# A fused attention and two-layer expert kernel: other step numbers for its planner, and two kinds of subtraction and rounding on other engines

## The chip, the cores and the metric

One Trainium2 chip, one of its cores. The metric is the device time of one execution in microseconds, the median of several runs; the kernel before has 794.7 us, median of three runs (794.32 to 796.21). Tensors lie in SBUF on 128 partitions; TensorE (PE, weight loads PEld) writes to PSUM; VectorE (DVE), ScalarE (ACT) and GpSimd (POOL) work between them; SyncE (SP) issues most DMAs.

## What is computed

Three layers one behind the other, on 1536 tokens (2 batches of 768) of 512 numbers:

```
attention, 8 heads of 64:  scores = q k' / 8, kept where the 6-bit hash of q equals that of k
                           (the signs of q @ proj and k @ proj), else -1e9; softmax; @ v
first layers:              h = x @ w_in (512 x 2048); g = h * sigmoid(1.702 h); x = g @ w_out (2048 x 512)
experts, 8 of 512x1024x512: logits = x @ w_gate + log1p(exp(x @ w_noise)) * noise; the two best per token,
                           softmax of the two; sum of weight * relu(x @ w1[e]) @ w2[e]
```

Matrices are split into a high and a low part of 16 bits, and a product is three matmuls: high by high, high by low, low by high.

## The kernel before, in words

**Steps.** The work is laid out in steps g, from about -17 to 116, in the loop of `fused` that ends with `by_turns`. Attention takes steps 0 to 95, one for each block of 128 queries of a head: batch b, chunk cc of 256 queries (three in a batch), pair hp of heads, head h and tile t. In a step come the score matmuls of step g+2 (`qk`, L259), the row maximum of step g+1 on VectorE (`rowmax`, L271), the exponential on ScalarE (`expo`, L280), and for steps under 24 a transpose on TensorE (`e_turn`, L298) and copies on ScalarE (L306). From step 24 on the probabilities are split into two 16-bit parts (`e_hi`, L319, ScalarE; `e_lo`, L328, VectorE) and transposed by a DMA (L332). `pv` (L373; L366 in the early steps) multiplies by the values some steps after a unit of four. A score tile has two PSUM buffers, so `qk` waits for the row maximum of two steps before.

**Keys and queries.** `stacks` puts the stages of one key or query tile on steps: `load`, `stack_hi` (rounding, L152; remainder on GpSimd, L154; scaled copy, L158 or L160), `stack_lo` (L167, and the DMA transpose L178), `buckets` (hash matmuls L195 and L196, copied to a tile `pc` by ScalarE, L200), `one_hot` (two comparisons on VectorE, L206) and `stack_end` (L213, and the second transpose L214). Their steps come from the tables KA (keys) and QA (queries); HE says which engine rounds, PC how many `pc` buffers there are. VA and VF set the steps of the values (`v_hi`, `v_lo`, `v_load32`).

**First layers.** The 32 weight blocks, 16 of `w_in` and then 16 of `w_out`, come as 8-byte numbers, 512 KB a block: `w_load` (L423), `w_bits` (three VectorE operations that make 4-byte numbers, L433, L436, L439), `w_split` (scaling on GpSimd, L452; high part on ScalarE, L455; low part on GpSimd, L456). Table W gives the step of each; its load comes two steps before. The raw numbers of the first 16 lie where the parts of `w_out` come later; those of the last 16 share three buffers (`wraw`). Each of six chunks of 256 tokens takes 16 steps behind its attention: in pieces 0 to 7 `moe_pe` computes h (L476), ScalarE takes a tanh (L494), VectorE multiplies (L506), ScalarE rounds (L520) and the lower part is subtracted (`moe_split`, L522) by the engine that GS names; in pieces 8 to 15 it multiplies by `w_out` (L487).

**Routing.** `route` computes the gate (L627, L629) of a chunk from rows transposed by a DMA (L589), some 30 small VectorE operations, and scatters the rows to the experts' slots in DRAM by indirect DMAs of GpSimd (L736). RA gives its first step, counted from the first step of the chunk. The slots are cleared beforehand from step I0 on, the output from step O0 on.

**Order.** Up to step 99 a planner of the language chooses each engine's order when the program is built: it takes what is ready by its own estimate of times, earlier steps first. Each engine then runs its instructions in that fixed order, each waiting for what it needs. From step 100 on the order is the program's. The experts come after step 116: `l1` (L854), `l1_out` (L864, L865), `l2` (L885, L879), `l2_out` (L895), and an indirect DMA that adds to the output (L902).

The tables are set like this (only the last update of W is quoted), and `stacks` uses them:

```
PARAM.update(W=[(g_,1) for g_ in [-6,-4,-2,0,2,3,4,5,7,8,9,10,12,13,14,15,17,18,19,20,20,21,21,22,22,23,23,24,24,25,25,26]])
...
        oh = PARAM["OH"]
        at(g - 2, load, nm, b, u)
        at(g, stack_hi, nm, b, u)
        soon(g + 1, stack_lo, nm, b, u)
        start(g + PARAM['BK'], buckets, nm, b, u)
        at(g + oh, one_hot, nm, b, u)
        soon(g + oh + 1, stack_end, nm, b, u)
```

Of the kernel before, what the change touches and what calls it, by code (L numbers as in the profile page):

```python
# [57 lines left out]
PARAM = dict(GM=16, HE=lambda nm, b: 'D', OE=lambda nm, b: 'D', SC=lambda nm, b: 'D', WB=0, XO=lambda b: 'D', NG=16, WS=lambda i: 'P', TS=lambda g: True, XL=lambda g: 'D', GW=2, E0=7, T0=12, T1=16, EL=8, WX=3, PV={(1,2,3):4}, PVD=5, ST={}, VA={}, RA={}, O0=48, OS=2, IS=2, FU=16, VF=2, EC=lambda g: 'AA', QX=8, QS=3, EA=1, S1=(8,8,8,9,9,9,11,13), QE=8, XG=2, XB=2, PC=2, OH=3, BK=3, R0=18, R1=0, LK=8, WL=1, NW=3, LE=lambda nc: nc.scalar, I0=24, LQ=8, LV=0, W=[(g, 1) for g in range(-6, 30)], KA={(0,0,0):-8,(0,0,1):-6,(0,1,0):-4,(0,1,1):-2}, QA={(0,0,0):-7,(0,0,1):-3}, HI=lambda g: 'P', LO=lambda g: False)  # L58
# [10 lines left out]


PARAM.update(W=[(g_,1) for g_ in [-6,-4,-2,0,2,3,4,5,7,8,9,10,12,13,14,15,17,18,19,20,20,21,21,22,22,23,23,24,24,25,25,26]])


@with_exitstack
# [1185 lines left out]
```

## Time and profile before

| what | value |
|---|---|
| median of 3 runs | 794.7 us (794.32 to 796.21) |
| the profiled execution | 792.2 us, span of its instructions 790.5 us |
| granted TensorE clock, mean | 0.976 of 2.4 GHz |
| busy: PE, DVE, ACT, POOL | 705.3, 496.9, 444.0, 282.1 us |
| row maxima of the 96 attention steps | 22.4 to 447.2 us |
| experts' matmuls | about 512 to 775 us |

The profile is of one execution. A busy time is the union of an engine's instructions in a stretch. A wait is the idle time of an engine before an instruction, put down to what ended it last. A granted clock of 0.50 is 1.2 GHz, of 1.00 is 2.4 GHz.

### The profile page before, as it was taken

To read this page: it belongs to the slowest core of one execution; us is meant where nothing else is said; L and a number is where in the kernel's file an instruction comes from. 1 tells how busy PE (TensorE), PEld (TensorE's weight loads), DVE (VectorE), ACT (ScalarE), POOL (GpSimd) and SP (SyncE) were. 2 spreads that over 40 slices of the span, in tenths; PEclk is the share of its full clock that TensorE was granted. 3 is DMA by queue.
4 is the path that set the end of the run, shared out by engine and by line. 5 is a ranking of instruction groups with operands and counts; after the bars stand their busy time and mean duration, and the time that the engine had idled before them with its cause. 6 is when DMAs were issued, how large, how long until landed. Compare 5 with 4: busy or idle time off the path is not lost.

```text
span 790.5 us, 14896 instructions
## 1 busy us (share of the span) xinstructions
PE 705.3 (89%) x5432; PEld 432.6 (55%) x5433; DVE 496.9 (63%) x1245; ACT 444.0 (56%) x958; POOL 282.1 (36%) x360
## 2 busy tenths in 40 slices
PE   1786689997888899889999999999999999999995
PEld 0453357555654575467557667466554545555452
DVE  8689689857985687378768725665643526345220
ACT  3678977657785686477658614445543534435220
POOL 7456856822462356114222224222031221302203
PEclk9999889999999999999999999999999999999998
DMA  8999657999999999975697580658977668484213
GB/s 196 224 250 317 195 175 167 274 255 171 170 198 194 170 194 217 177 137 103 117 178 133 107 290 11 187 194 209 280 120 242 193 121 267 61 255 85 27 17 45
DMA packets 254973, 136.83 MB, mean 173 GB/s; under 512 B 211696, under 2 KB 230704, under 8 KB 254896
## 3 DMA queue, kind: packets, MB, share of 16 engines
q1 hardware_dynamic: 248880, 122.68, 66.3%
q0 software_dynamic: 6016, 13.16, 9.4%
q8 instruction: 43, 0.70, 0.3%
q14 instruction: 34, 0.28, 0.1%
HBM read 62.27 MB, written 23.20 MB: 108 GB/s over the span
## 4 chain that ended last, share of the span: by engine, by line
PE 44%; DVE 4%; issue 1%; DMA 1%; ACT 1%; POOL 1%; POOLq 0%; DVEq 0%; ACTq 0%
PE ph L854 15%; PE py L885 14%; PE px L487 7%; PE h L476 3%; DMA et<-er 1%; PE pv L373 1%; PE py L879 1%; PE s L259 1%; DVE er L328 1%; POOL out_dram L902 1%; DVE ew L794 1%; DVE th L506 0%; ACT er L319 0%; DVE e L271 0%; ACT ew L793 0%
## 5 line engine op out<-in xcount | busy, mean ns | idle before, releaser
L476 PE MATMUL h<-xt,wi 128*128 128x256 f16 x1152 | 136.9, 274 | 5.9 <-DVE th L506 4.0
L487 PE MATMUL px<-wo,gt 128*128 128x512 f16 x576 | 133.2, 384 | 2.0 <-ACT wo L455 1.1
L854 PE MATMUL ph<-xg,ew 128*128 128x400 f16 (+2 forms) x864 | 132.8, 314 | 1.0 <-DVE ht L865 1.0
L794 DVE SCALAR_TENSOR_TENSOR ew<-w,ew 128x1024 f16<-128x1024 f32 x64 | 77.8, 1225 | 83.3 <-ACT ew L793 83.3
L885 PE MATMUL py<-ew,ht 128*128 128x512 f16 x576 | 126.0, 379 | 0.0
L476 PEld LDWEIGHTS <-wi 128*128 128x128 f16 x1152 | 111.9, 98 | 25.3 <-issue 8.0
L902 POOL DMA_INDIRECT out_dram<-yo,ti x32 | 54.0, 1687 | 200.5 <-ACT yo L895 190.9
L259 PE MATMUL s<-kt,qt 128*128 128x512 f16 (+3 forms) x384 | 84.3, 340 | 31.7 <-DVE e L271 24.3
L854 PEld LDWEIGHTS <-ew 128*128 128x128 f16 x864 | 80.4, 98 | 51.0 <-issue 2.8
L328 DVE SCALAR_TENSOR_TENSOR er<-e,mx,er 128x768 f16<-128x768 f32 x68 | 71.6, 1055 | 51.2 <-ACT er L319 50.2
L522 POOL TENSOR_TENSOR gt<-th,gt 128x512 f16<-128x512 f32 x48 | 57.0, 1188 | 105.5 <-ACT gt L520 105.5
L885 PEld LDWEIGHTS <-ht 128*128 128x128 f16 x576 | 56.1, 98 | 67.0 <-issue 0.2
L271 DVE TENSOR_SCALAR_CACHE_REDUCE e<-s 128x768 f32<-128x768 f32 x96 | 90.5, 948 | 3.2 <-PE pt L298 1.3
L487 PEld LDWEIGHTS <-gt 128*128 128x128 f16 x576 | 55.5, 98 | 66.4 <-issue 5.4
L280 ACT ACTIVATE e<-e,mx 128x768 f32<-128x768 f32 x96 | 89.4, 931 | 1.8
L319 ACT ACTIVATE er<-e,mx 128x768 f16<-128x768 f32 x68 | 63.1, 930 | 36.1 <-DMA et<-er 28.2
L895 ACT ACTIVATE yo<-py,wv 128x512 f32<-128x512 f32 x24 | 16.5, 687 | 94.6 <-PE py L885 57.9
L259 PEld LDWEIGHTS <-qt 76*128 76x128 f16 (+1 forms) x384 | 35.0, 100 | 61.2 <-issue 26.7
L793 ACT ACTIVATE ew<-w 128x1024 f16<-128x1024 f32 x64 | 66.2, 1048 | 0.1
L864 ACT ACTIVATE ht<-ph 128x400 f16<-128x400 f32 (+2 forms) x72 | 33.4, 465 | 57.7 <-PE ph L854 57.1
L865 DVE SCALAR_TENSOR_TENSOR ht<-ph,ht 128x400 f16<-128x400 f32 (+2 forms) x72 | 37.5, 523 | 30.7 <-ACT ht L864 30.6
L373 PE MATMUL pv<-et,vt 128*64 128x256 f16 x648 | 44.0, 277 | 6.5 <-DMA et<-er 6.3
(233 smaller groups left out, 918.8 us busy)
## 6 DMA issues: line engine op xcount, KB each, us to landing
w<-in_moe_w_dram SPq DMA_DIRECT2D x64, 512.0 KB, 5.4
wo<-in_moe_w_in_dram SPq DMA_DIRECT2D x16, 512.0 KB, 5.1
wraw<-in_moe_w_out_dram SPq DMA_DIRECT2D x16, 512.0 KB, 5.0
slots<-blank SPq DMA_DIRECT2D x6, 1032.0 KB, 6.3
v<-in_v_dram SPq DMA_DIRECT2D x28, 192.0 KB, 4.1
out_dram<-zeros SPq DMA_DIRECT2D x13, 256.0 KB, 3.3
k<-in_k_dram SPq DMA_DIRECT2D x16, 192.0 KB, 2.9
q<-in_q_dram SPq DMA_DIRECT2D x24, 128.0 KB, 2.9
```

The costliest lines, as they stand in the source:

```text
L259: nc.tensor.matmul(ps[:, n0 * 128:n1 * 128], qt[:kr, s, h, t, :], kt[:kr, s, h, n0:n1, :].rearrange("p c t -> p (c t)"), start=(s == 0), s ...
L271: nc.vector.tensor_scalar(e32, st[g]["ps"][:, :S], -FAR, -TOP, op0=OP.max, op1=OP.max, accum_out=mx[:, 0:1])
L280: nc.scalar.activation(e32, e32, AF.Exp, scale=0.125, bias=st[g]["mx"][:, 1:2], accum_out=sms[b, cc, hp][:, 2 * h + t:2 * h + t + 1] if g ...
L319: nc.scalar.activation(er[:, 0], st[g]["e"], AF.Copy, scale=r)
L328: nc.vector.scalar_tensor_tensor(er[:, 1], d["e"], d["mx"][:, 3:4], er[:, 0], op0=OP.mult, op1=OP.subtract)
L476: nc.tensor.matmul(ph[:, a, :], wi[ws][:, d, f0:f0 + 128], xt[:, d, xs, :], start=(d == 0 and ws == 0 and xs == 0), stop=(d == HP - 1 and ...
L487: nc.tensor.matmul(px, gts[ci, f // 2][:, gs, f % 2, t * 128:t * 128 + 128], wo[ws][:, f, :], start=(f == 0 and gs == 0 and ws == 0), stop ...
L793: nc.scalar.activation(hi, x, AF.Copy, scale=SW1 if j == 0 else SW2)
L794: nc.vector.scalar_tensor_tensor(lo, x, SW1 if j == 0 else SW2, hi, op0=OP.mult, op1=OP.subtract)
L854: nc.tensor.matmul(ph[:, :c1 - c0], w[:, ws, d * FE + f * 128:d * FE + f * 128 + 128], xg[e, p][:, xs * HP + d, :], start=(d == 0 and ws = ...
L885: nc.tensor.matmul(py, ht[:, f, hs, t * 128:t * 128 + 128], w[:, ws, f * DM:(f + 1) * DM], start=(i == 0), stop=(i == n - 1))
L902: ins = nc.gpsimd.indirect_dma_start(out=dst, out_offset=bass.IndirectOffsetOnAxis(ap=ti[:np_, o:o + 1], axis=0), in_=yo[:np_, :nd], in_of ...
```

## The change

It adds three updates of the table of parameters behind the last one. What differs by them:

- **KA**, first batch's keys (pair, head): (0,0) from step -15 to -12, (0,1) -6 to -5, (1,0) -5 to -9, (1,1) -4 to -2. **QA**: four query tiles one step, (0,0,1) to -4, (0,1,1) to 10, (1,0,0) to 38, (1,1,2) to 61.
- **W**: blocks 0 to 7 keep their steps; blocks 8 to 15 go from 7, 8, 9, 10, 12, 13, 14, 15 to 6, 7, 7, 8, 10, 11, 12, 13; blocks 16 to 31 from 17, 18, 19, 20, 20, 21, 21, 22, 22, 23, 23, 24, 24, 25, 25, 26 to 15, 17, 17, 18, 20, 20, 20, 20, 21, 22, 22, 23, 23, 25, 25, 26.
- **VA** (0,0,0) -1 to -2, (0,1,0) -1 to 2, (1,1,1) -4 to -3, and **VF** 0 to -1, the early values one step later. **PV**: (0,0,2) 6 to 5, (0,0,3) 5 to 4, (0,1,2) 4 to 5, (0,1,3) 5 to 4, (1,2,0) 6 to 4.
- **RA**: the routing of chunks 0 to 4 from 18, 18, 19, 24, 18 to 20, 19, 18, 21, 19. **I0** 26 to 28, **O0** 56 to 57. **PC** 2 to 1.
- **GS**: the lower parts of pieces 5, 6, 7 of chunk 1, pieces 0, 4, 5, 6, 7 of chunk 2 and pieces 0 to 3 of chunk 3 on VectorE, the other 36 on GpSimd as before. **HE**: the second batch's eight key tiles rounded by GpSimd.

The other entries repeat what stood there. The function LO differs at steps 29 and 42 alone, where it isn't called.

```diff
+PARAM.update(PC=1)
+
+PARAM.update(KA={(0, 0, 0): -12, (0, 0, 1): -5, (0, 1, 0): -9, (0, 1, 1): -2, (0, 2, 0): -1,
...
+RA={0: 20, 1: 19, 2: 18, 3: 21, 4: 19},ST={0: 4, 1: 4, 2: 5, 3: 4, 4: 5, 5: 3},
+W=[(g_,1) for g_ in [-6, -4, -2, 0, 2, 3, 4, 5, 6, 7, 7, 8, 10, 11, 12, 13, 15, 17, 17, 18, 20, 20, 20, 20, 21, 22, 22, 23, 23, 25, 25, 26]],
+O0=57,I0=28,GW=2,WL=2,BK=3,T0=12,T1=17,R1=2,VF=-1,OH=3,
+XS=lambda nm,b:'PPPPPP'[2*"qkv".index(nm)+b],SC=lambda nm,b:'DADD'[2*"qkv".index(nm)+b],
+HE=lambda nm,b:'DPDP'[2*"qkv".index(nm)+b],KC=lambda nm,b:'DPPP'[2*"qkv".index(nm)+b],
+GS=lambda ci,i:'PPPPPPPPPPPPPDDDDPPPDDDDDDDDPPPPPPPPPPPPPPPPPPPP'[8*ci+i],XN='P',
...
+PARAM.update(QA=dict(PARAM['QA']) | {(0,1,3):21,(1,2,3):84,(0,1,0):8,(0,1,1):10})
```

## Rows read from the trace of the kernel before

**Rows 1.** Busy by stretch: us, busy us (x instructions) of PE, PEld, DVE, ACT, POOL, clock, DMA.
```profile
22.40:120.90 98.50, 73.61 (x545) 46.08 (x546) 82.42 (x191) 76.87 (x203) 60.80 (x77) 0.90 0.88 229
120.90:480.00 359.10, 328.13 (x2793) 219.37 (x2792) 253.78 (x670) 236.14 (x540) 134.51 (x142) 0.99 0.88 179
...
511.70:774.80 263.10, 261.77 (x1783) 143.61 (x1783) 122.53 (x285) 107.75 (x172) 54.75 (x66) 1.00 0.63 160
```

**Rows 2.** Waits, whole span: engine, line, waited for; us in total, times, longest us.
```profile
PE s L259 <- DVE e L271: 24.3, 20, 4.8
...
DVE pfi L433 <- DMA wraw<-in_moe_w_out_dram: 6.7, 4, 4.4
...
PE pv L373 <- DMA et<-er: 6.3, 6, 2.3
```

**Rows 3.** Timeline of VectorE near 98 us: start, us, what [idle before <-releaser].
```profile
98.57 0.69 DVE L433 TENSOR_SCALAR pfi<-wraw 128x512 int32<-128x512 int32 x1 [4.42 <-DMA wraw<-in_moe_w_out_dram]
...
99.91 0.95 DVE L271 TENSOR_SCALAR_CACHE_REDUCE e<-s 128x768 f32<-128x768 f32 x1
```

**Rows 4.** Timeline of TensorE near 100 us.
```profile
100.92 1.44 PE L259 MATMUL s<-kt,qt 128*128 128x512 f16 x4 [4.80 <-DVE e L271]
```

**Rows 5.** SyncE's queue, 66 to 100 us: first and fourth load into the raw buffers.
```profile
66.41 0.57 SPq L423 DMA_DIRECT2D wraw<-in_moe_w_out_dram  x1
...
93.15 0.37 SPq L423 DMA_DIRECT2D wraw<-in_moe_w_out_dram  x1
```

**Rows 6.** Line L433 by itself: ns min/median/max, first to last start.
```profile
L433 DVE TENSOR_SCALAR pfi<-wraw x16: 674/692/715, 83.3 to 157.5; 128x512 int32<-128x512 int32 x16
```

**Rows 7.** Timeline of GpSimd near 92 us.
```profile
91.79 1.16 POOL L456 TENSOR_TENSOR wo<-wraw,wo 128x512 f16<-128x512 f32 x1
```

**Rows 8.** Line L271 by itself, columns as in rows 6.
```profile
L271 DVE TENSOR_SCALAR_CACHE_REDUCE e<-s x96: 925/948/958, 22.4 to 447.2; 128x768 f32<-128x768 f32 x96
```

**Rows 9.** Busy by stretch, columns as in rows 1: two half-clock stretches, one near 290 us.
```profile
97.80:104.60 6.80, 3.68 (x27) 2.60 (x27) 5.87 (x15) 5.02 (x13) 3.90 (x6) 0.50 0.55 197
...
278.70:282.10 3.40, 3.40 (x18) 2.41 (x16) 3.40 (x10) 2.77 (x9) 2.87 (x3) 0.50 1.07 196
...
285.80:300.70 14.90, 14.10 (x149) 11.40 (x148) 14.25 (x46) 12.51 (x31) 8.84 (x9) 1.00 1.00 199
```

**Rows 10.** Timeline of TensorE near 278 us: the second chunk's gate.
```profile
278.28 0.27 PE L627 MATMUL pz<-wg,xrt 128*128 128x32 f16 x4 [2.02 <-DMA xrt<-xr]
```

**Rows 11.** SyncE's queue near 346 us: the third chunk's second transpose.
```profile
346.02 1.41 SPq L589 DMA_TRANSPOSE xrt<-xr  x1
```

**Rows 12.** Timeline of TensorE near 357 us: the third chunk's gate.
```profile
357.49 0.25 PE L627 MATMUL pz<-wg,xrt 128*128 128x32 f16 x4
```

**Rows 13.** SyncE's queue at the start: first query and first weight block.
```profile
1.30 0.42 SPq L129 DMA_DIRECT2D q<-in_q_dram  x1
...
3.05 0.59 SPq L423 DMA_DIRECT2D wo<-in_moe_w_in_dram  x1
```

**Rows 14.** Timeline near 15 us: second bucket copy, first comparisons.
```profile
14.25 0.20 ACT L200 ACTIVATE pc<-s 128x48 f32<-128x48 f32 x1
...
15.44 0.74 DVE L206 TENSOR_TENSOR ks<-pc 128x36 f16<-128x36 f32 x2
```

**Rows 15.** Groups by line: names, shapes, count | busy us, mean ns | idle before.
```profile
L522 POOL TENSOR_TENSOR gt<-th,gt 128x512 f16<-128x512 f32 x48 | 57.0, 1188 | 105.5 <-ACT gt L520 105.5
...
L152 POOL TENSOR_SCALAR qsb<-q 128x256 f16<-128x256 f32 x12 | 13.8, 1150 | 23.0 <-DMA q<-in_q_dram 22.2
...
L152 DVE TENSOR_SCALAR ks<-k 128x384 f16<-128x384 f32 x16 | 8.2, 515 | 5.2 <-DMA k<-in_k_dram 3.1 <-issue 1.5 <-DMA kt<-ks 0.6
...
L326 DVE TENSOR_TENSOR er<-e,er 128x768 f16<-128x768 f32 x3 | 2.9, 954 | 0.4 <-ACT er L319 0.4
```

**Rows 16.** Timeline of VectorE near 209 us.
```profile
208.73 0.97 DVE L695 TENSOR_TENSOR d<-top 128x2 f32<-128x2 f32 x1
```

**Rows 17.** Timeline of GpSimd near 209 us.
```profile
208.49 1.20 POOL L522 TENSOR_TENSOR gt<-th,gt 128x512 f16<-128x512 f32 x1 [4.10 <-ACT gt L520]
```

More of the change, by code (lines that the diff above doesn't have):

```diff
@@ L71 @@
 PARAM.update(W=[(g_,1) for g_ in [-6,-4,-2,0,2,3,4,5,7,8,9,10,12,13,14,15,17,18,19,20,20,21,21,22,22,23,23,24,24,25,25,26]])
+PARAM.update(PC=1)
+PARAM.update(KA={(0, 0, 0): -12, (0, 0, 1): -5, (0, 1, 0): -9, (0, 1, 1): -2, (0, 2, 0): -1, (0, 2, 1): 1, (0, 3, 0): 4, (0, 3, 1): 5, (1, 0, 0): 37, (1, 0, 1): 39, (1, 1, 0): 44, (1, 1, 1): 46, (1, 2, 0): 42, (1, 2, 1): 51, (1, 3, 0): 47, (1, 3, 1): 51},QA={(0, 0, 0): -15, (0, 0, 1): -4, (0, 0, 2): 1, (0, 0, 3): 3, (0, 1, 0): 10, (0, 1, 1): 9, (0, 1, 2): 17, (0, 1, 3): 19, (0, 2, 0): 24, (0, 2, 1): 28, (0, 2, 2): 30, (0, 2, 3): 33, (1, 0, 0): 38, (1, 0, 1): 41, (1, 0, 2): 47, (1, 0, 3): 52, (1, 1, 0): 57, (1, 1, 1): 56, (1, 1, 2): 61, (1, 1, 3): 69, (1, 2, 0): 72, (1, 2, 1): 69, (1, 2, 2): 80, (1, 2, 3): 82},VA={(0, 0, 0): -2, (0, 0, 1): -3, (0, 1, 0): 2, (0, 1, 1): -1, (0, 2, 0): 0, (0, 2, 1): 0, (0, 3, 0): -1, (0, 3, 1): -2, (1, 0, 0): -1, (1, 0, 1): -1, (1, 1, 0): 2, (1, 1, 1): -3, (1, 2, 0): -3, (1, 2, 1): -3, (1, 3, 0): 2, (1, 3, 1): -2},PV={(0, 0, 0): 4, (0, 0, 1): 5, (0, 0, 2): 5, (0, 0, 3): 4, (0, 1, 0): 6, (0, 1, 1): 4, (0, 1, 2): 5, (0, 1, 3): 4, (0, 2, 0): 5, (0, 2, 1): 5, (0, 2, 2): 5, (0, 2, 3): 6, (1, 0, 0): 4, (1, 0, 1): 5, (1, 0, 2): 4, (1, 0, 3): 5, (1, 1, 0): 5, (1, 1, 1): 5, (1, 1, 2): 5, (1, 1, 3): 6, (1, 2, 0): 4, (1, 2, 1): 4, (1, 2, 2): 4, (1, 2, 3): 4},RA={0: 20, 1: 19, 2: 18, 3: 21, 4: 19},ST={0: 4, 1: 4, 2: 5, 3: 4, 4: 5, 5: 3},W=[(g_,1) for g_ in [-6, -4, -2, 0, 2, 3, 4, 5, 6, 7, 7, 8, 10, 11, 12, 13, 15, 17, 17, 18, 20, 20, 20, 20, 21, 22, 22, 23, 23, 25, 25, 26]],O0=57,I0=28,GW=2,WL=2,BK=3,T0=12,T1=17,R1=2,VF=-1,OH=3,XS=lambda nm,b:'PPPPPP'[2*"qkv".index(nm)+b],SC=lambda nm,b:'DADD'[2*"qkv".index(nm)+b],HE=lambda nm,b:'DPDP'[2*"qkv".index(nm)+b],KC=lambda nm,b:'DPPP'[2*"qkv".index(nm)+b],GS=lambda ci,i:'PPPPPPPPPPPPPDDDDPPPDDDDDDDDPPPPPPPPPPPPPPPPPPPP'[8*ci+i],XN='P',WS=lambda i:'pppppppppppppppppppppppppppppppp'[i],EC=lambda g:2*'AAAAAAAAAAAAAAAA'[g%16],HI=lambda g:'AAAAAAAAAAAAAAAAAAAAAAAAAAAAAAAAAAAAAAAAAAAAAAAAAAAAAAAAAAAAAAAAAAAAAAAAAAAAAAAAAAAAAAAAAAAAAAAA'[g],LO=lambda g:'DPDPDPDPDPDPDPDPDPDPDDDPDDDPDPDPDDDPDDDPDDPPDDDPDDDPDDDPDDDPDDDPDDDPDDDPDDDPDDDPDDDPDDDPDDDPDDDP'[g]=="P")
+PARAM.update(QA=dict(PARAM['QA']) | {(0,1,3):21,(1,2,3):84,(0,1,0):8,(0,1,1):10})
 @with_exitstack
```

## The prediction

> **What bounds the kernel now.** I read the busy time of each engine by stretch first, to see where TensorE stands idle; then the waits, for who held it; then the timelines of the engines around the longest of those waits. From 511.7 to 774.8 us, the experts, TensorE is busy 261.8 of 263.1 us: nothing the change moves can show there except by starting that stretch sooner or later. From 120.9 to 480 us it idles 359.1 - 328.1 = 31.0 us, and from 22.4 to 120.9 us 98.5 - 73.6 = 24.9 us, at a granted clock of 0.90 [rows 1]. So some 56 us is what any new order can win, nearly half of it in the first fifth of the time, where VectorE is busy 82.4 of 98.5 us. Most of the TensorE wait has one cause: score matmuls wait 24.3 us for VectorE's row maximum (L271), which frees their PSUM tile [rows 2].
>
> The largest single case is the one to follow. VectorE stands still 4.42 us until 98.57, because the next instruction in its order is the bit conversion of a weight block whose load has not landed; the row maximum queued behind it starts at 99.91 [rows 3]; TensorE resumes at 100.92 after 4.80 us [rows 4]. Why was the load late? The second-layer blocks have three raw buffers. The first of them was loaded from 66.41, but VectorE converted the first only from 83.3 [rows 5, 6], and GpSimd took its lower part at 91.79 for 1.16 us, to 92.95 [rows 7]; the load into that buffer could start only at 93.15 [rows 5]. So a block that is converted late makes a load late three blocks on.
>
> **The change part by part.** Steps before step 100 are priorities for a planner, not fixed places; I treat a step as the time between row maxima, (447.2 - 22.4) / 95 = 4.5 us [rows 8].
>
> *Weight blocks.* Blocks 16 to 19 move two, one, two and two steps forward (17, 18, 19, 20 to 15, 17, 17, 18). Two steps are 9 us: the first buffer comes free near 84 instead of 92.95, its load of 5.4 us (93.15 to 98.57 [rows 3, 5]) lands near 89.5, before VectorE wants it at 94.15. The 4.42 us go. Bounds: all waits of VectorE for these loads are 6.7 us [rows 2], so -6.7 below; above, the wait is repeated, +4.8 [rows 4], since four blocks now share step 20 with three buffers. I take -4.4, the row that the moved blocks touch. What is late next is the row maximum's own work: the conversions that move forward stand before row maxima of steps 15 to 18 and no longer before those of 19 and 20; their number is unchanged, so I cost the shift itself at nothing, hidden as long as VectorE has the 16.1 us idle of that stretch [rows 1]. Blocks 8 to 15 move one or two steps forward into the same stretch: also nothing. The stretch from 97.8 to 104.6 us ran at half clock [rows 9], after TensorE had idled; TensorE does not set the pace there, so no gain is counted.
>
> *Routing.* The steps go from 18, 18, 19, 24, 18 to 20, 19, 18, 21, 19. The second chunk's gate matmul waits 2.02 us at 278.28 for the transposed row [rows 10]; one step more, 4.5 us, covers it: -2.0. The 3.4 us of half clock that follow it, with TensorE busy throughout [rows 9], would give another 1.7; other idle times were not always followed by such a stretch, so that is a bound (-3.7), not the value. The third chunk's routing, one step earlier, has its transpose issued at 346.02 and its matmul at 357.49 [rows 11, 12]: 11.5 us of room for a step of 4.5, so nothing; if the room fails, +2.0, the wait of the second chunk. The fourth is three steps earlier and cannot pass its transpose; the fifth is one later in the hand-written part, bounded by one step, which only matters if an expert's rows then arrive late. Nothing for both.
>
> *First keys, one bucket buffer.* The first key load now stands behind the first query and two projection loads: issue time 3.05 - 1.30 = 1.75 us later [rows 13]. The second pair of keys goes ahead of the first pair's second head, so that head's transpose is one place further back on the SP queue. With a single bucket buffer the copy at 14.25 waits until VectorE has read the first one, 15.44 + 0.74 = 16.18: 1.93 us [rows 14]; ScalarE's work behind it waits as long. Both together are 3.7 us, one end; the other is a gain of 1 us, as the first query comes sooner. VectorE has conversions to do meanwhile, so less than half reaches the end: +1.5.
>
> *Gated lower parts and second keys.* Twelve of 48 subtractions leave GpSimd, 12 x 1.188 = 14.3 us, for VectorE, where the same subtraction over 768 columns takes 954 ns, so 512 columns 0.64 us: +7.6 us. Eight key roundings leave VectorE, 8 x 0.515 = 4.1 us, for GpSimd, where 256 columns take 1150 ns, so 384 some 1.73 us: 13.8 us [rows 15]. Sum: VectorE +3.5 us, GpSimd -0.5 us. VectorE idles 359.1 - 253.8 = 105 us between 120.9 and 480 [rows 1]: taken as nothing. The ends are -4.1 (only the key roundings count, all before row maxima that TensorE awaits) and +8.4, the slower rival below.
>
> *The rest.* Probability-value products move by at most two steps; all their waits for the transposed probabilities are 6.3 us, the longest 2.3 [rows 2]: nothing, +/-2.3. Values and the clearing transfers move one to three steps in a stretch where they are early: nothing. The lambdas for rounding, copying and lower parts of the probabilities return what they returned, at every step at which they are called.
>
> **Sum:** -4.4 - 2.0 + 1.5 = -4.9 us. On the profiled execution, 792.2 us (span 790.5 and 1.7 around it), that is 787.3. The median of the runs shown is 794.7, 2.5 above it; the forecast on the median is 794.7 - 4.9 = 789.8.
>
> **A rule that speaks against it.** At 208.73 a two-input VectorE operation on 128x2 numbers takes 0.97 us and ends at 209.70; GpSimd's gated subtraction, begun at 208.49, ends at 209.69 [rows 16, 17]. So VectorE stood until GpSimd was done.
> The Trainium skill, page "SBUF — State Buffer", section "Who interferes with whom", says that a VectorE instruction with two SBUF inputs and a GpSimd instruction that reads SBUF exclude each other for the whole instruction; by that rule, with which this row agrees, each of the twelve new VectorE subtractions can wait for GpSimd too.
>
> **The rivals.**
> (a) *The wait only moves.* Four blocks at step 20 on three buffers: the fourth load waits for the first block's lower part, and VectorE stands 4.4 us before it. Then -4.9 + 4.4 = -0.5: 794.2. For it: a load takes 5.4 us, one of the three conversion steps only 0.69 [rows 3]. The same figure follows if the planner orders these conversions as before, so that the change does not do what it says. Against: the first three are no longer late.
> (b) *The port decides: slower.* Four of the moved subtractions (third chunk, pieces 4 to 7) fall between 285.8 and 300.7 us, where VectorE is busy 14.25 of 14.90 us [rows 9]. Four cost 2.5 us and, each meeting a GpSimd operation of 1.19 us, 4.8 more: 7.3 - 0.65 of slack = 6.7 us; a row maximum held over 2 us brings a half-clock stretch of 3.4 us [rows 9], 1.7 more: +8.4. Time: 794.7 - 4.9 + 8.4 = 798.2; without the gain in the weight blocks 802.6. It decides as soon as VectorE's slack in that stretch is gone. Against: four subtractions leave GpSimd in just that stretch, so there is less to meet.
> (c) *More than the one wait goes.* Blocks 8 to 15 moved forward even out VectorE's order from step 6 on, and half of the other 24.9 - 4.8 = 20.1 us of TensorE idle goes too: -10 more, 779.8.
>
> **How the numbers follow.** A measurement of this kernel tells about 0.3%, 2.4 us, from no change. Forecast 0.47, own range 785 to 793; (c) 0.12; (a) 0.15; (b) 0.18; the start's +3.7 with the wait kept, also slower, 0.08. A tenth of the forecast's chance lies within 0.3%. So faster 0.54, same 0.20, slower 0.26. The range goes from (c), 779, to (b) without the gain, 803.
>
> **What would show it.** Right: no VectorE wait of over 2 us for a second-layer load before step 24, TensorE idle from 22.4 us to step 24 near 20 us, no wait for the second chunk's transposed row, the experts' first matmul some 5 us earlier. Wrong: a VectorE wait for a load of 4 us elsewhere (a), VectorE full near 290 us and TensorE waiting there for row maxima (b), or a first row maximum later than 24 us.

## The result, and the profile after

The changed kernel takes 783.65 us (median of 4 runs, 782.32 to 785.66), the kernel before 794.51 us on the same chip (4 runs): a ratio of 0.987, 95% interval 0.9831 to 0.9909, so 10.9 us faster where 4.9 were forecast. The profiled execution shown here took 784.4 us, its span 782.4.

Busy time by stretch, changed kernel; the columns are those of [rows 1], and the first, second and fourth line answer to its three stretches.

```profile
22.40:120.90 98.50, 75.74 (x544) 48.06 (x545) 84.22 (x186) 77.07 (x202) 61.01 (x77) 0.84 0.90 232
120.90:480.00 359.10, 334.55 (x2895) 228.13 (x2893) 263.61 (x705) 242.43 (x553) 134.66 (x144) 1.00 0.82 180
280.00:300.00 20.00, 18.99 (x174) 14.24 (x173) 19.29 (x66) 17.60 (x44) 5.42 (x6) 1.00 0.97 214
511.70:774.80 263.10, 260.52 (x1765) 140.35 (x1763) 115.52 (x243) 105.52 (x158) 54.51 (x71) 1.00 0.61 149
```

TensorE's idle time falls from 31.0 to 359.1 - 334.55 = 24.6 us in the long middle, and only from 24.9 to 22.8 us in the front, where its granted clock is lower than before (0.84 against 0.90). So the gain does not lie where the prediction looked for it. The row maxima say the same: step 24's begins at 123.9 us against 120.9 before, 3.0 later, but the last of the 96 at 433.1 against 447.2 [rows 8].

```profile
L279 DVE TENSOR_SCALAR_CACHE_REDUCE e<-s x96: 939/948/959, 22.1 to 433.1; 128x768 f32<-128x768 f32 x96
```

The waits over the whole span (us in total, times, longest), changed kernel:

```profile
ACT er L327 <- DMA et<-er: 22.0, 19, 4.5
PE s L267 <- DVE e L279: 17.7, 18, 3.7
PE pv L381 <- DMA et<-er: 6.9, 7, 1.6
...
DVE pfi L441 <- DMA wraw<-in_moe_w_out_dram: 2.2, 4, 1.0
```

TensorE's wait for row maxima fell from 24.3 to 17.7 us, VectorE's for second-layer loads from 6.7 to 2.2 [rows 2]. ScalarE's wait to write the next probabilities until a DMA transpose has read the old ones, which the prediction had not looked at, is 22.0 us; in the kernel before it was 29.4:

```profile
ACT er L319 <- DMA et<-er: 29.4, 18, 4.8
```

Timelines of the changed kernel: the start, VectorE near 97 us (the place of [rows 3]), two probability-value products, the second chunk's gate ([rows 10]), the experts' first matmul.

```profile
14.35 0.20 ACT L208 ACTIVATE pc<-s 128x48 f32<-128x48 f32 x1
16.00 0.21 ACT L208 ACTIVATE pc<-s 128x72 f32<-128x72 f32 x1
...
22.15 0.95 DVE L279 TENSOR_SCALAR_CACHE_REDUCE e<-s 128x768 f32<-128x768 f32 x1
...
96.78 0.86 DVE L441 TENSOR_SCALAR pfi<-wraw 128x512 int32<-128x512 int32 x1 [0.74 <-DMA wraw<-in_moe_w_out_dram]
...
192.24 2.15 PE L381 MATMUL pv<-et,vt 128*64 128x256 f16 x35 [0.88 <-DMA et<-er]
...
209.73 2.13 PE L381 MATMUL pv<-et,vt 128*64 128x256 f16 x35 [1.59 <-DMA et<-er]
...
270.76 0.27 PE L635 MATMUL pz<-wg,xrt 128*128 128x32 f16 x4 [1.43 <-DMA xrt<-xr]
...
501.91 1.45 PE L862 MATMUL ph<-xg,ew 128*128 128x256 f16 x9 [2.33 <-DMA xg<-slots]
```

The 4.42 us of VectorE are 0.74. The second copy of buckets stands at 16.00 instead of 14.25 (it is now the first key's, 128x72, where it was the first query's, 128x48), and the first row maximum is no later for it (22.15; 22.4 before). The gate still waits 1.43 of 2.02 us. The experts now begin with a wait of 2.33 us for their rows that the kernel before did not have; the clock is at half for 3.4 us behind it. From the last gated product (px) to the same expert matmul some 190 us on it takes 190.4 us instead of 186.4. The experts' first matmul is still 9.7 us earlier than before (501.9; 511.6).

The groups that the engine moves touch, with the columns of [rows 15]:

```profile
L530 POOL TENSOR_TENSOR gt<-th,gt 128x512 f16<-128x512 f32 x36 | 43.6, 1211 | 89.1 <-ACT gt L528 88.6
L160 POOL TENSOR_SCALAR ks<-k 128x384 f16<-128x384 f32 x8 | 13.1, 1635 | 0.6
L530 DVE TENSOR_TENSOR gt<-th,gt 128x512 f16<-128x512 f32 x12 | 9.0, 753 | 0.8 <-ACT gt L528 0.7
```

### The profile page after: what moved, and what is told of

The parts are those of the page before. It is cut to its first block, busy times and chain, and to the rows that moved or that the text cites. A ratio compares the mean times of both kernels' runs of the same rounds, so it can differ in the third digit from the quotient of the medians.

```text
span 782.4 us, 14895 instructions
## 1 busy us (share of the span) xinstructions
PE 704.6 (90%) x5432; PEld 435.8 (56%) x5433; DVE 497.6 (64%) x1249; ACT 445.3 (57%) x958; POOL 275.3 (35%) x356
## 4 chain that ended last, share of the span: by engine, by line
PE 37%; DVE 5%; issue 3%; DMA 3%; ACT 2%; POOL 1%; SPq 0%; POOLq 0%; DVEq 0%; ACTq 0%
PE ph L862 16%; PE py L893 14%; PE px L495 3%; PE h L484 2%; PE py L887 2%; DMA et<-er 1%; DVE e L279 1%; DVE er L336 1%; POOL slots L744 1%; DMA slots<-xr,si 1%; ACT er L327 1%; PE pv L381 1%; DMA xg<-slots 1%; DVE ew L802 1%; DVE th L514 0%
## 5 line engine op out<-in xcount | busy, mean ns | idle before, releaser
L484 PE MATMUL h<-xt,wi 128*128 128x256 f16 x1152 | 133.8, 272 | 3.8 <-DVE th L514 2.2
L495 PE MATMUL px<-wo,gt 128*128 128x512 f16 x576 | 130.0, 379 | 2.0 <-DVE th L514 2.0
L484 PEld LDWEIGHTS <-wi 128*128 128x128 f16 x1152 | 111.0, 98 | 21.7 <-issue 5.9
L910 POOL DMA_INDIRECT out_dram<-yo,ti x32 | 50.1, 1565 | 204.3 <-ACT yo L903 192.5
L267 PE MATMUL s<-kt,qt 128*128 128x512 f16 (+3 forms) x384 | 87.6, 348 | 24.9 <-DVE e L279 17.7
L893 PEld LDWEIGHTS <-ht 128*128 128x128 f16 x576 | 56.3, 98 | 66.8 <-issue 0.2
L530 POOL TENSOR_TENSOR gt<-th,gt 128x512 f16<-128x512 f32 x36 | 43.6, 1211 | 89.1 <-ACT gt L528 88.6
L267 PEld LDWEIGHTS <-qt 128*128 128x128 f16 (+1 forms) x384 | 35.9, 102 | 55.9 <-issue 20.8
```

Source lines behind the costliest of these rows:

```text
L267: nc.tensor.matmul(ps[:, n0 * 128:n1 * 128], qt[:kr, s, h, t, :], kt[:kr, s, h, n0:n1, :].rearrange("p c t -> p (c t)"), start=(s == 0), s ...
L484: nc.tensor.matmul(ph[:, a, :], wi[ws][:, d, f0:f0 + 128], xt[:, d, xs, :], start=(d == 0 and ws == 0 and xs == 0), stop=(d == HP - 1 and ...
L495: nc.tensor.matmul(px, gts[ci, f // 2][:, gs, f % 2, t * 128:t * 128 + 128], wo[ws][:, f, :], start=(f == 0 and gs == 0 and ws == 0), stop ...
L893: nc.tensor.matmul(py, ht[:, f, hs, t * 128:t * 128 + 128], w[:, ws, f * DM:(f + 1) * DM], start=(i == 0), stop=(i == n - 1))
```

## The experiments

The theory after the result was that of the prediction, with other sizes: shorter waits at the moved weight blocks and routing steps. The rival: the part costed at a loss, first keys and one bucket buffer, carries the gain. Runs 1 to 4 take one part back out of the changed kernel. All ratios are to the kernel before on the same chip, with 95% intervals; the changed kernel is 783.65, 0.987. The new steps of the values and of the probability-value products, and the first clearing step (I0), were not tried by themselves.

**1. Old steps for the weight blocks, in the changed kernel.**
```diff
+PARAM.update(W=[..., (17,1), (18,1), (19,1), (20,1), ...])
```


> The changed kernel with the weight blocks on their old steps. Theory 1 (the weight steps carry the gain by removing the wait of VectorE for the fourth second-layer load): about 788 us, some 4.4 us of the 10.9 lost, and a VectorE wait of about 4 us for such a load is back before step 24. Theory 2 (the two engine moves carry it, between steps 28 and 72): 784, no loss. Theory 3 (no part carries it; the planner's whole order is new with any edit): anything from 782 to 792, and the orders differ far beyond the weight blocks.

789.19 us, 0.9938 (0.9914 to 0.9962): 5.5 us of the gain are lost. VectorE's wait for a second-layer load is back, 3.8 us at its longest, as theory 1 had it. But step 24's row maximum begins at 123.4 us, no later than with the new steps (123.9), and TensorE idles as long from 125 to 450 us (22.6 us; 22.5 with the new steps). What differs there is four stretches of half clock (124, 202, 274, 298 us) where the changed kernel's profile has none. The old steps cost time, but not through the wait in the front.

**2. Old routing steps.**
```diff
+PARAM.update(RA={0: 18, 1: 18, 2: 19, 3: 24, 4: 18})
```


> The changed kernel with routing on its old steps 18, 18, 19, 24, 18. Theory 1: 785 to 786, the wait of TensorE for the second chunk's transposed row goes from 1.4 to some 2 us, but the 2.3 us wait before the first expert goes away, since the fifth chunk's routing is a step earlier: together about 784. Theory 2: 784. Theory 3: 782 to 792.

783.1 us, 0.986 (0.9842 to 0.9878): nothing is lost. The wait for the first expert's rows is gone, and the stretch that took 190.4 us takes 186.4 again, so as much is lost elsewhere; where is not shown. The second chunk's gate waits 0.99 us with the old step, less than with the new one (1.43), against the expectation. The five steps together are worth nothing.

**3. Old engines: second keys rounded on VectorE, all gated lower parts on GpSimd.**
```diff
+PARAM.update(HE=lambda nm,b:'DPDD'[2*(nm=='k')+b], GS=lambda ci,i:'P')
```


> The changed kernel with all gated lower parts on GpSimd and the second batch's keys rounded by VectorE, as before. Theory 1: 784, these moves cost and bring nothing. Theory 2: 790 or more, TensorE's idle time between 172 and 251 us goes from 6 back to about 14 us, with a half-clock stretch. Theory 3: 782 to 792.

786.77 us, 0.9925 (0.99 to 0.9951): the moves are worth some 3.1 us here, near what this measurement can tell. From 172 to 251 us TensorE idles 9.9 us (6.4 in the changed kernel), with half clock from 199 and from 251 us: part of what theory 2 expected.

**4. Old steps for keys and queries, and two bucket buffers.**
```diff
+PARAM.update(KA={(0,0,0): -15, ...}, QA={...}, PC=2)
```


> The changed kernel with the old steps of keys and queries and two bucket buffers. Theory 1: 782, the start is some 1.5 us earlier and the rest as it is. Theory 2: 782 to 784. Theory 3: 782 to 792, and the first 24 steps change in either direction.

795.03 us, 1.0007 (0.9988 to 1.0025): the whole gain is lost. The part that was costed at +1.5 us carries it. All three theories had 792 us or less.

**5. The fifth chunk's routing alone back, from step 19 to 18.**
```diff
+PARAM.update(RA=dict(PARAM['RA']) | {4: 18})
```


> The changed kernel with only the fifth chunk's routing back one step, 19 to 18; it lies in the part whose order is written by hand, so the planner's part is the same. If the 2.3 us wait of TensorE for the first expert's rows and the 3.4 us at half clock behind it come from this step: 779 to 781, and no such wait. If the wait comes from the scatters' end whatever the step: 783 to 784 with the wait kept.

781.18 us, 0.9828 (0.9806 to 0.985): 2.5 us faster than the change itself. TensorE goes from the gate straight into the experts:

```profile
499.65 0.24 PE L640 MATMUL pz<-wg,xrt 128*128 128x16 f16 x4
...
499.75 1.47 PE L865 MATMUL ph<-xg,ew 128*128 128x256 f16 x12
```

**6. In the kernel before: new steps for keys and queries, one bucket buffer, nothing else.**
```diff
+PARAM.update(KA={...}, QA={...}, PC=1)
```


> The kernel before with the new steps of keys and queries and one bucket buffer alone. If these steps carry the gain (taking them back cost 11 us): 784 to 786. If the gain belongs to the order as a whole (theory 3): 790 to 798, and the longest TensorE waits between 120 and 450 us again reach 2 us or more, with half-clock stretches.

781.73 us, 0.9859 (0.9837 to 0.9881): this part alone gives the whole gain. The signs named for the other theory are there all the same: TensorE's longest wait between 120 and 450 us is 2.76 us, and four stretches of half clock lie there. They do not tell a fast kernel from a slow one.

**7. A control in the kernel before: the clearing transfers one step later.**
```diff
+PARAM.update(O0=57)
```


> A control: the kernel before with only the clearing of the output one step later (56 to 57), transfers that nothing waits for. If orders respond to specific parts only: 794, within 1 us. Theory 3: up to 4 us either way, since the planner reorders 162 lines of VectorE's list for it.

792.83 us, 0.9985 (0.9962 to 1.0007): no difference that can be told. It is a weaker control than expected: position by position, the two traces differ in 26 of VectorE's 1245 instructions, not 162 (with one bucket buffer, run 9, in 137). This small reordering at least is worth nothing.

**8 and 9. The bucket buffer by itself:** two buffers in the changed kernel, and one buffer in the kernel before.
```diff
+PARAM.update(PC=2)
...
+PARAM.update(PC=1)
```


> The changed kernel with two bucket buffers again. My step for the single buffer (a wait of 1.9 us at the start, +1.5 together with the keys): 782 to 783, the first row maxima earlier by 1 to 2 us. Theory 3: 780 to 790, whichever way the order falls after the first steps.

> The kernel before with one bucket buffer instead of two, nothing else. Theory A (the single buffer carries the gain: two buffers in the changed kernel lost it all): 782 to 785. Theory B (steps of keys and queries together with the buffer, as one order): 790 to 796. The prediction's own step: 1 to 2 us slower than before, 795 to 796, from a later copy at the start.

Two in the changed kernel: 794.01 us, 1.0004 (0.9982 to 1.0026), all of the gain lost. One in the kernel before: 782.24 us, 0.9844 (0.9818 to 0.987), all of it there. A buffer that is *taken away* makes the kernel 10 to 12 us faster. With two, the first row maximum of the changed kernel is 0.4 us earlier (21.7; 22.1), not 1 to 2. The profile with two buffers in the changed kernel shows where; these timeline lines stand at the same places as 192.24 and 209.73 above:

```profile
194.09 2.15 PE L384 MATMUL pv<-et,vt 128*64 128x256 f16 x35 [2.88 <-DMA et<-er]
...
212.16 3.18 PE L384 MATMUL pv<-et,vt 128*64 128x256 f16 x35 [2.62 <-DMA et<-er]
```

The waits for the transposed probabilities are 2.88 and 2.62 us instead of 0.88 and 1.59. Is that another order? Not here: from 115.5 to 273.9 us of the changed kernel every engine has the same instructions in the same order with either buffer count, and VectorE's 310 of them take 160.1 us with one buffer and 166.6 with two. In the kernel before the pair is cleaner still: all five engines have one order from the start to about 275 us, but for one swap on ScalarE near 52 us, ahead of the windows, and one in the last 2 us of them. Windows of the same 422 VectorE instructions (the other engines' counts differ by a record or two at the edges, TensorE's by records that are missing), first with two buffers (the kernel before),

```profile
52.90:280.00 227.10, 188.87 (x1573) 122.62 (x1573) 178.30 (x422) 163.21 (x391) 116.72 (x136) 0.96 0.94 211
```

then with one (run 9):

```profile
52.90:274.10 221.20, 188.23 (x1590) 123.11 (x1589) 178.45 (x422) 163.69 (x393) 115.30 (x136) 0.96 0.92 217
```

The same work (178.30 and 178.45 us of VectorE) at the same granted clock takes 227.1 us with two buffers and 221.2 with one. One kernel profiled twice (runs 6 and 11) differs by 0.5 us over this stretch. And one buffer less can only add waits for a buffer. So something else than order or a wait for buffers is slower with two. Waits over the whole span, changed kernel with two buffers:

```profile
ACT er L330 <- DMA et<-er: 35.2, 22, 4.9
...
PE pv L384 <- DMA et<-er: 11.3, 6, 2.9
```

Both sums are greater than with one (22.0 and 6.9). In the kernel before, one buffer leaves ScalarE's sum nearly where it was (28.7 us; 29.4 with two), but TensorE's own wait falls from 6.3 to 2.1 us, as the group of line L376 (L373 of the kernel before) shows:

```profile
L376 PE MATMUL pv<-et,vt 128*64 128x256 f16 x648 | 43.2, 275 | 3.1 <-DMA et<-er 2.1 <-DVE xt L402 0.9
```

The page's third part says that the transfers themselves take longer. The same packets and bytes, and the time that they took as a share of 16 engines' span: the kernel before, then the changed kernel with two buffers,

```profile
q1 hardware_dynamic: 248880, 122.68, 66.3%
...
q1 hardware_dynamic: 248880, 122.68, 66.2%
```

and with one buffer, the kernel before (run 9) and the changed kernel alike:

```profile
q1 hardware_dynamic: 248880, 122.68, 65.0%
```

The control of run 7, with two buffers, has 66.8%. So I counted the trace's packet records. Of the 196,608 packets of 256 B, which are those of the transposes, the median takes 18 ns in every kernel. A second group takes 20 to 59 ns. The table gives that group, then all the packets that follow a transpose of each kind (a packet is put down to the last transpose issued over 1 us before it, so neighbours blur a little). Beside it stands where the tiles that are transposed (er, xr) or written by a transpose (kt) begin in a partition of SBUF, as bytes past a multiple of 256; that is read from the built programs.

```
kernel                  pc bufs  er at  et<-er          xr at    xrt<-xr      kt at  kt<-ks      us
before                     2      32    17167/99034    128,160  1947/11993     0   1449/27153  794.5
7 control                  2      32    16729/98192    128,160  2173/11828     0   1231/26541  792.8
10 key steps, two          2      32    17714/102190   128,160  2115/11915    64   1346/29220  788.1
8 changed, two             2      32    17345/94519    128,160  2273/13308    64   1429/29244  794.0
4 keys back, two           2      32    15547/98616    128,160  2110/10887     0   1030/27161  795.0
9 before, one              1       0     1623/105238   128,160  1559/9826      0    659/26399  782.2
6 keys alone, one          1       0     1579/104146   128,160  1715/10345    32    730/24378  781.7
changed                    1       0     1648/99774    128,160  1682/11212    32    868/26224  783.7
```

A bucket buffer is 288 bytes in each partition, and the probabilities (er) stand behind it in the same pool. With two buffers they begin 32 bytes past a multiple of 256, with one exactly on it. With two, 16 to 18% of the packets behind their transposes take 20 ns or more, with one 1.5 to 1.7%; the six other profiles with one buffer have 1.3 to 2.1%. The routing rows (xr) begin off a multiple of 256 in every kernel, and the packets behind their transposes are slow in 15 to 19% of the cases (12 to 19% over all profiles).

The blur can be taken out by counting: up to the experts 72 transposes of probabilities have 1536 of these packets each, 32 of keys 768, 48 of queries 512 and 11 of rows 1024, and the experts' 25,600 make up the rest of the 196,608. Dealt out in the order of issue, no packet starts before its transpose is issued. Counted so, 15.6 to 17.8% of the probabilities' packets are slow with two buffers and 1.2 to 1.9% with one, and from its first packet to the end of its last such a transpose takes 2.01 to 2.02 us (median of 72) in the five profiles with two buffers, 1.57 to 1.64 us in the nine with one. So each of these transposes is some 0.4 us longer.

Is it the place of the source or of the destination? The probabilities cannot tell, for their destination (et) lies behind the bucket buffers too and moves with the source: 32 past a multiple of 256 with two buffers, on it with one. The rows' destination (xrt) is off as well, at 192 and 224. The keys can tell one side: their sources lie on a multiple of 256 in every kernel, while their destination kt begins at 0, 32 or 64, and by the count 2.8 to 3.3% of their packets are slow at 0, 3.0 to 4.1% at 32, 3.1 to 3.4% at 64. A destination off the multiple alone does not make one packet in six slow. That speaks for the place of the source; a source off the multiple with its destination on it is in none of these kernels.

**10. The new key and query steps without the single buffer, in the kernel before.**
```diff
+PARAM.update(KA={...}, QA={...})
```


> The kernel before with the new steps of keys and queries, two bucket buffers as before. Theory A: 793 to 796, no gain without the single buffer. Theory B: 788 to 796. If the steps alone carry it: 781 to 784. In any case the idle time of TensorE between 125 and 450 us plus half of the half-clock time there should rank this run: near 36 us for 794, near 25 for 782.

788.13 us, 0.9925 (0.9903 to 0.9948). The steps by themselves win 6.4 us; with one buffer (run 6) the same steps are 6.4 us faster still. TensorE's idle time plus half of the half-clock time, 27.9 + 3.4 = 31.3 us, does lie between the two marks. But run 9, which is faster, has 25.6 + 3.4 = 29.0 us and not 25, so the measure ranks only roughly. With two buffers the probabilities have as many slow packets here as before (17.5% by the count; 17.2%), so these 6.4 us come from somewhere else.

**11. The kernel of run 6 once more.**

> A second look at the kernel before with keys, queries and one bucket buffer alone, as in the earlier run of it, for how far one kernel's profile differs from its own: 780 to 785, the idle time of TensorE between 125 and 450 us within 3 us of the 18.5 seen.

The kernel is line for line that of run 6. A single execution took 782.79 us (run 6: 781.73), with TensorE idle for 18.8 us from 125 to 450 us (18.5).

**12. Run 6 and the engine moves.**
```diff
+PARAM.update(KA={...}, QA={...}, PC=1, HE=..., GS=...)
```


> The kernel before with keys, queries, one bucket buffer, and the two engine moves. Added effects (the engine moves were worth 3 us in the changed kernel): 778 to 779. Theory 3 (parts don't add): 779 to 790.

781.33 us, 0.9842 (0.9821 to 0.9863): on top of run 6 the engine moves are worth nothing that can be told.

Runs 5, 6, 9 and 12 are all 1.4 to 1.7% faster than the kernel before and 1.4 to 2.5 us faster than the changed kernel; their intervals overlap, so none is the best, and over the changed kernel they gain about what a measurement can tell. The smallest of them is run 9: one buffer instead of two.

**What is shown and what is not.** Shown by runs 8 and 9: the single buffer makes the difference in either kernel. Shown by the traces of these two pairs, one profile of each kernel: 5.9 us of the 7.5 between the profiled spans of the first pair (before, run 9), and 6.5 of 9.2 for the changed kernel, are lost in stretches where every engine's order is the same; the medians differ by 12.3 and 10.4, and no profile shows where the difference lies. Shown by the packet records of all the kernels: where the probabilities and their transposed tiles begin goes, without exception, with how many slow packets their transposes have and how long these take; shared out over 16 engines the 256-byte packets take 294.8 us before and 281.6 changed. That the place is the cause of these 6 us is the likeliest reading, not a test: every tile behind the bucket buffers moves with them, and a kernel that moves the probabilities by some bytes and keeps orders and buffers was not tried. The rest of what the profiles show comes behind 275 us, where the buffer count also reorders the second chunk's routing (the kernel before had two bucket copies there at once); place and order aren't told apart there.

## Why the prediction was right or wrong

The direction was right. The time, 783.65 us, lies below the forecast's own 785 to 793 and inside the whole range, 779 to 803, but the sum was not made of the right terms: the largest gain came from the one part that was booked as a loss. That the time fell into the range is luck.

**First keys, one bucket buffer (+1.5): the step that failed.** "With a single bucket buffer the copy at 14.25 waits until VectorE has read the first one" came true nearly to the number. With the buffer alone (run 9) ScalarE stands 1.91 us before that copy (1.93 predicted):

```profile
16.69 0.21 ACT L203 ACTIVATE pc<-s 128x48 f32<-128x48 f32 x1 [1.91 <-PE s L199]
```

TensorE, which the line names, had been done at 14.60; VectorE's comparison of the first buffer ended at 16.57. It cost little at the first row maximum (22.9; 22.4 before, in the changed kernel 22.15). What the step left out is everything else that a buffer count does. It gave a gain of at most 1 us as its lower end; the runs show -12.3 for the buffer alone (run 9) and -12.8 with the steps (run 6). No row that I read of the kernel before named the place of a tile, but its trace had a hint: ScalarE's 29.4 us and TensorE's 6.3 us of waiting for the same transposes, of which the sum took TensorE's alone, and asked only whether steps would move it.

**Weight blocks (-4.4): the wait went, the gain did not come with it.** VectorE's 4.42 us became 0.74, and its longest wait for a second-layer load is 1.0 us. But not by the way that was forecast. "Two steps are 9 us: the first buffer comes free near 84" failed: in the changed kernel VectorE converts the first second-layer block at 82.42 (83.3 before), GpSimd takes its lower part at 90.87 (91.79), and the load into that buffer starts at 92.06 (93.15), one microsecond sooner instead of nine.

```profile
82.42 0.69 DVE L441 TENSOR_SCALAR pfi<-wraw 128x512 int32<-128x512 int32 x1
...
90.87 1.16 POOL L464 TENSOR_TENSOR wo<-wraw,wo 128x512 f16<-128x512 f32 x1
...
92.06 0.33 SPq L431 DMA_DIRECT2D wraw<-in_moe_w_out_dram  x1
```

VectorE starts on the fourth block 1.8 us sooner (96.78; 98.57), and it came to wait only at 96.04 instead of 94.15, with other work until then; that is how 3.7 us of the wait went. And step 24's row maximum begins 3.0 us later, not 4.4 sooner: TensorE's longest wait for a row maximum is still 3.7 us (4.8 before), now up to 86.7 us, while VectorE works through conversions and a query's rounding, and the front has more half clock. Run 1 puts the new steps at 5.5 us, but in places that the step did not name.

**Routing (-2.0): wrong.** The gate's wait went to 1.43 us, not to nothing, and with the old step (run 2) it is 0.99: one step later was not the 4.5 us of cover that it was counted as. "Which only matters if an expert's rows then arrive late" described the fifth chunk rightly, and they did: 2.33 us of wait, 2.5 us by run 5, booked at nothing. The five steps together are worth nothing (run 2).

**Gated lower parts and second keys (0): right within what can be told.** The prices were near (key rounding 1.635 us on GpSimd for 1.73; the subtraction 753 ns on VectorE for 640). Near 290 us VectorE is full, 19.29 of 20 us, as rival (b) said, but TensorE is busy 18.99: the row maxima were not held, so (b) falls. The twelve moved subtractions take 668 to 1171 ns: the excess over the shortest is 12 x (753 - 668) = 1.0 us. Two of them began while GpSimd was at a subtraction of its own, and took 1010 and 1171 ns; the other ten took 668 to 693.
The rule of the Trainium skill, page "SBUF — State Buffer", section "Who interferes with whom", that was weighed in the prediction agrees with these two, but they are few.

**Rivals.** (a) falls in its time, for the wait did not come back; but its second condition, that the planner orders these conversions as before, came near the truth, as the times of the first block show. (c) came nearest in time (779.8), but not by its mechanism: idle time in the front fell by 2.1 us, not by ten more.

**The parts do not add.** Taken back one at a time, they cost 5.5, -0.5, 3.1 and 11.4 us, 19.5 in all, where the change is worth 10.9; run 6 alone gives at least as much as everything. Separate terms are the wrong form where a planner makes the orders anew with each change.

## What to carry to other kernels

A changed buffer count or tile size is also a change of place for every tile behind it in the pool: before costing the wait for the missing buffer, look where the sources and destinations of DMA transposes then begin, and compare the DMA queue's time for the same packets. Cost a wait by all the engines that have it, not only by the one that bounds the kernel; and where a planner reorders everything, put each part alone into the old kernel as well as taking it out of the new one, since the two give different sums.

## What the runs showed of the hardware that was not expected

**The place of a transpose's source.** Where source and destination of a transpose both begin off a multiple of 256 bytes (the probabilities at 32 and 32, the rows at 128 or 160 and 192 or 224), about one 256-byte packet in six takes 20 ns or more instead of 18; with both on the multiple, one in sixty of the probabilities' packets. With the destination alone off it (the keys of the changed kernel) it is 4.1%, against 2.8 to 3.3% of the keys' packets with both on it. No kernel here has the source alone off it.
The Trainium skill, page "DMA: Bandwidth & Descriptors", section "How a descriptor splits into AXI transactions", says that a transaction must start from a 256-byte boundary, and that a descriptor which does not begin on one is cut so that bytes below it are fetched too. The packet records agree with the direction; that most such packets are as fast as the others it does not say.

**Half clock.** TensorE's granted clock fell to half for 3.4 us at a time in the middle of the kernel before (at 224, 279 and 323 us, where TensorE had waited 2.87, 2.02 and 2.62 us) and never there in the changed kernel's profile, whose longest wait between 125 and 450 us is 1.83 us. A wait of 2.28 us before was not followed by one, nor one of 2.77 us in run 9. In 3.4 us at half clock a TensorE that is busy throughout does the work of 1.7, so a wait of two microseconds can cost up to 1.7 more, and this, too, makes separate terms not add.

**Scatter.** Executions of one kernel lie up to 7 us from its median (before, in the four of the first comparison: 791.35 to 796.21), so that a single profile can mislead: that of run 4 took 788.3 us where the kernel's median is 795.0.
